# Turning the third weight of a feed-forward block in 32x32 blocks on VectorE instead of on TensorE

## The chip, the core and the metric

The kernel runs on one core of a Trainium2 chip. The core has five engines that run at the same time, each with its own list of instructions in a fixed order: TensorE (PE in the profile; its weight loads are PEld), VectorE (DVE), ScalarE (ACT), GpSimd (POOL) and SyncE (SP), which here only issues DMAs. They wait for each other through semaphores. The metric is the device time of one execution in microseconds.

## What is computed

A gated linear recurrence over 4 batches, 8 heads, 768 steps and head width 48, and then a feed-forward block on its output, x, of 3072 tokens by 384:

```python
for t in range(S):
    state = alpha[:, :, t, :, None] * state + np.einsum('bhd,bhe->bhde', k[:, :, t], v[:, :, t])
    y[:, :, t] = np.einsum('bhd,bhde->bhe', q[:, :, t], state)
...
a = x @ w1
b = x @ w2
h = a * b @ w3
return (h @ w_out).astype(np.float32)
```

w1 and w2 are 384 x 1024, w3 is 1024 x 1024, w_out is 1024 x 384. The four weights come to the kernel as 64-bit floats; everything else is 32-bit.

## The kernel before

**Stages.** The first part, until about 186 us, works the recurrence off in 24 chunks of 128 tokens (N) and stores x, transposed, to DRAM in eight groups of three chunks (`xd`). The second part, the gates, multiplies x by w1 and w2 for 8 groups of 384 tokens and 8 tiles of 128 of the 1024 columns, 64 gates in all, and stores each product ab to DRAM (`abd`). Twenty gates already run inside the first part (`early_gate`), the other 44 follow (`late_gate`). The third part (`project`, from about 370 us) loads ab again and multiplies it by one matrix of 1024 x 384. That matrix, `w3o`, is w3 times w_out: the kernel does not multiply ab by w3 and the result by w_out, it folds the two weights together first. The fold is done in eight steps of 128 rows of w3 (`fold(i)`), spread among the late gates.

**Products in three parts.** TensorE multiplies values cut to a short mantissa (FP32R), so each operand is split into parts h, l and m: h is the value rounded down by a ScalarE activation, l and m are what is left, made by two VectorE instructions. A product of K tiles takes 3 x K matmuls. `onto` does the first two parts into one PSUM bank, has ScalarE scale the bank in place (L535), and adds the third part later, when two more products have been begun (`pending`, `settle(keep)`). A late gate is two such products of nine matmuls each (KM = 3): the first is copied to a tile r by ScalarE (L567), and VectorE multiplies the second bank by r into ab (L571). r has two buffers, PSUM has eight banks.

**Weights.** `to_fp32` turns 64-bit floats into 32-bit ones by integer work. It loads a `raw` tile (four buffers) through SP's queue (L230), then ScalarE makes `rest` of the low words (L238) and `power` (L243), and VectorE does five instructions: two masks or shifts of the high words (L239, L242), two scalar_tensor_tensor (L245, L246) and a multiplication (L248). `load_out(j)` converts 128 rows of w_out and splits them into `wo` (L590 to L594), `load_w3(i, c0)` converts 128 rows by 512 columns of w3 into half of a tile `w3`, which has three buffers. These generators stand in a queue, `weights`; `fetch` starts the loads ahead and `convert` advances the conversions by a step or two at each gate. A DMA on a queue waits, before it is issued, until the eighth before it has landed, because eight semaphores go round.

**The fold.** A product with w3 contracts over w3's columns, while w3 lies with its rows on the partitions. So `fold(i)` first transposes 128 rows of w3: eight 128x128 transposes on TensorE into two PSUM banks (L612), from which ScalarE writes h (L614) and VectorE l and m (L615, L618) of `w3T`, a tile with a single buffer. Then `onto` multiplies w3T by wo: 16 matmuls for the first two parts, 8 for the third. `done` splits the result into w3o (L623 to L625).

**Order.** The Python loops give each engine's work, and a scheduler in the framework puts the instructions of every engine in a fixed order when the program is built. The main loop over `todo`, the list of gates, interleaves a gate, some steps of conversion and, once two loads of a fold's w3 are converted, that fold. Between the start of one fold's products and the next lie 54 matmuls of gates and 24 of the fold. Splits of x for the groups that come next (`split_x`, L502 to L504) stand in between, and the stores of ab and the loads of x go through GpSimd's queue in this part.

Of the kernel before, what the change touches and what calls it, by code (L numbers as in the profile page):

```python
# [10 lines left out]
FP32 = mybir.dt.float32  # L11
# [4 lines left out]
AF = mybir.ActivationFunctionType  # L16
ALU = mybir.AluOpType
# [3 lines left out]
P = 4096.0  # L21
# [27 lines left out]
def kernel(  # L49
# [12 lines left out]
    nc = tc.nc  # L62
    B, H, S, D = q.shape
    C = 128
    DM = H * D
    DF = moe_w1.shape[1]
    NCH = S // C
    N = B * NCH
    NP = H // 2
    DP = 64  # L70
    KM = DM // C
    KF = DF // C
    G = 3
# [2 lines left out]
    CW = 512  # L76
# [3 lines left out]
    TURNED = 8  # L80
    assert D <= DP and DM % C == 0 and DF % CW == 0 and S % C == 0 and N % G == 0
    assert DM <= 512 and TG <= 512

    def pool(name, bufs, stack=ctx, **kw):
        return stack.enter_context(tc.tile_pool(name=name, bufs=bufs, **kw))
# [19 lines left out]
    def bank():  # L105
        return ps.tile([C, 512], FP32, tag="bank", name="bank")

    st, mark = {}, {}
# [13 lines left out]

    vs = [p1.tile([C, H, DP], FP32, name=f"v{i}") for i in range(AHEAD + 1)]
    for x in vs:
        nc.gpsimd.memset(x[:, :, D:], 0.0)
    vts = [p1.tile([C, NP, DP], FP32, name=f"vt{i}") for i in range(2)]
    for x in vts:
# [35 lines left out]
    def turn_v(n):  # L163
        if turned(n):
            for half in range(2):
                nc.gpsimd.tensor_copy(out=vts[n % 2][ds(DP * half, DP), :, 0:D],  # L166
                                      in_=st["v", n][ds(DP * (1 - half), DP), 1::2, 0:D])

    spare = tr[0].tile([C, 3 * KM * TG], FP32R, tag="x3", name="x3")[:].bitcast(FP32)
    sums2 = spare[:, 0:4 * C].rearrange("p (e s t) -> p e s t", e=2, s=2)  # L170
# [11 lines left out]
    ident = const.tile([C, C], FP32, name="ident")  # L182
    rebias = const.tile([C, 1], FP32, name="rebias")

    w12 = [p.tile([C, 3, 2, KM, CW], FP32R, name=f"w12{i}") for i, p in enumerate((w12ap, const))]

# [5 lines left out]
    keep = p1.tile([C, C], I32, name="keep")  # L192
    keep_turned = p1.tile([C, 2, DP], I32, name="keep_turned")
    qks = [p1.tile([C, 2, H, DP], FP32, name=f"qk{i}") for i in range(3)]
# [27 lines left out]
    for x in Ts + decs:  # L222
        nc.gpsimd.memset(x, 0.0)

    def to_fp32(dst, *srcs):

        n, m = len(srcs) * srcs[0].shape[1], srcs[0].shape[1]
        raw = rawp.tile([C, n], I64, tag="raw", name="raw")
        for i, src in enumerate(srcs):
            nc.sync.dma_start(out=raw[:, ds(i * m, m)], in_=src)  # L230
        yield
        words = raw.bitcast(U32).rearrange("p (n w) -> p n w", w=2)
        low, high = words[:, :, 0], words[:, :, 1]

        mant = cvt.tile([C, n], FP32, tag="mant", name="mant")
        top = mant.bitcast(U32)
        rest = cvt.tile([C, n], FP32, tag="rest", name="rest", bufs=2)
        nc.scalar.activation(rest, low, AF.Copy, scale=2.0 ** -52)  # L238
        nc.vector.tensor_scalar(top, high, 0x000FFFFF, 0x00100000, op0=ALU.bitwise_and, op1=ALU.bitwise_or)  # L239

        power = cvt.tile([C, n], U32, tag="power", name="power", bufs=2)
        nc.vector.tensor_scalar(power, high, 20, 0x7FF, op0=ALU.logical_shift_right, op1=ALU.bitwise_and)  # L242
        nc.scalar.activation(power, power, AF.Relu, scale=2.0 ** 23, bias=rebias)  # L243
        yield
        nc.vector.scalar_tensor_tensor(mant, top, 2.0 ** -20, rest, op0=ALU.mult, op1=ALU.add)  # L245
        nc.vector.scalar_tensor_tensor(power, high, 0x80000000, power, op0=ALU.bitwise_and, op1=ALU.bitwise_or)  # L246
        to = mant if dst is None else dst()
        nc.vector.tensor_mul(to, mant, power.bitcast(FP32))  # L248
        yield
        return to  # L250

    def load_gates(i, kk, half):
        w = yield from to_fp32(None, (moe_w1, moe_w2)[i][ds(kk * C, C), ds(half * CW, CW)])
        h, l, m = (w12[half][:, x, i, kk, :] for x in range(3))
        nc.scalar.activation(h, w, AF.Copy, scale=(1.0 - 2.0 ** -13) / P)
        yield
        mark["l"] = nc.vector.scalar_tensor_tensor(l, h.bitcast(FP32), -P, w, op0=ALU.mult, op1=ALU.add).ins
        done.append((i, kk, half))
        if half:
            nc.vector.scalar_tensor_tensor(m, h.bitcast(FP32), P + 1.0, w, op0=ALU.mult, op1=ALU.subtract)  # L260
        else:
            thirds.append((m, h, l))

    weights, begun, thirds, done = deque(), deque(), deque(), []
# [229 lines left out]
    def load_x(g, queue=nc.sync):  # L494
        st["xT", g] = xp.tile([C, KM, TG], FP32, tag="xT", name="xT")
        queue.dma_start(out=st["xT", g], in_=xd[g].rearrange("(k p) t -> p k t", p=C))

    def split_x(g, i):
        x = st.pop(("xT", g))
        t = tr[i].tile([C, 3 * KM * TG], FP32R, tag="x3", name="x3").rearrange("p (s k t) -> p s k t", s=3, k=KM)  # L500
        st["x3", g] = t
# [29 lines left out]
    def onto(w, x, width, done, keep):  # L531

        p, n = bank()[:, 0:width], len(w[0])
        products(p, w, x, (0, 1), n, True, True)
        nc.scalar.activation(p, p, AF.Copy, scale=1.0 + 1.0 / P)  # L535

        def end():
            products(p, w, x, (2,), n, False, True)
            done(p)

        pending.append(end)
        settle(keep)

    def factors(g, f):
        x = [[st["x3", g][:, part, kk, :] for kk in range(KM)] for part in range(3)]
        half, at = divmod(f * C, CW)
        return [([[w12[half][:, part, i, kk, ds(at, C)] for kk in range(KM)] for part in range(3)], x)
                for i in range(2)]
# [36 lines left out]
            (nc.gpsimd if late else nc.sync).dma_start(out=abd[g][:, f, :], in_=ab)  # L585

    def load_out(j):
        w = yield from to_fp32(None, moe_w_out[ds(j * C, C), :])
        h, l, m = (wo[:, part, j, :] for part in range(3))
        nc.scalar.activation(h, w, AF.Copy, scale=1.0 - 2.0 ** -13)  # L590
        nc.vector.tensor_sub(w, w, h.bitcast(FP32))
        yield
        nc.scalar.activation(l, w, AF.Copy, scale=P)
        nc.vector.scalar_tensor_tensor(m, w, -P, h.bitcast(FP32), op0=ALU.mult, op1=ALU.add)  # L594

    def load_w3(i, c0):
        def to():
            if ("w3", i) not in st:
                st["w3", i] = foldp.tile([C, DF], FP32, tag="w3", name="w3", bufs=3)
            return st["w3", i][:, ds(c0, CW)]  # L600
        yield from to_fp32(to, moe_w3[ds(i * C, C), ds(c0, CW)])
        if c0 + CW == DF:
            folds.append(fold(i))

    def fold(i):
        w3 = st.pop(("w3", i))
        w3T = foldp.tile([C, 3, KF, C], FP32R, tag="w3T", name="w3T")
        rest = []
        for part in range(2):
            tp = bank().rearrange("p (j c) -> p j c", c=C)  # L610
            for j in range(KF // 2):
                nc.tensor.transpose(tp[:, j, :], w3[:, ds((part * KF // 2 + j) * C, C)], ident)  # L612
            h, l, m = (w3T[:, x, part * KF // 2:(part + 1) * KF // 2, :] for x in range(3))
            nc.scalar.activation(h, tp, AF.Copy, scale=1.0 - 2.0 ** -13)  # L614
            nc.vector.tensor_sub(l, tp, h.bitcast(FP32))  # L615
            rest.append((m, h, tp))
        for m, h, tp in rest:
            nc.vector.scalar_tensor_tensor(m, h.bitcast(FP32), -1.0 - 1.0 / P, tp, op0=ALU.mult, op1=ALU.add)  # L618
        yield True

        def done(po):
            h, l, m = (w3o[:, part, i, :] for part in range(3))
            nc.scalar.activation(h, po, AF.Copy, scale=(1.0 - 2.0 ** -13) / P)  # L623
            nc.vector.scalar_tensor_tensor(l, h.bitcast(FP32), -P, po, op0=ALU.mult, op1=ALU.add)
            nc.vector.scalar_tensor_tensor(m, h.bitcast(FP32), P + 1.0, po, op0=ALU.mult, op1=ALU.subtract)  # L625

        onto(*([[x[:, part, j, :] for j in range(KF)] for part in range(3)] for x in (w3T, wo)), DM, done, 2)
# [37 lines left out]
    for half in range(DF // CW):  # L665
        for kk in range(KM):
            weights.extend(load_gates(i, kk, half) for i in range(2))
# [21 lines left out]
    for n in range(N + 1):  # L689
# [89 lines left out]
        if n == N - 3:  # L779
            while begun:  # L780
                convert(1)
            weights.extend(load_out(j) for j in range(KF))
            fetch(4)
# [7 lines left out]
    foldp = pool("foldp", 1, stack=folding, reuse_waits="tile")  # L791
# [1 line left out]
    w3o = None  # L793
    folds, folded = deque(), 0
    for i in range(KF):
        for c0 in range(0, DF, CW):
            weights.append(load_w3(i, c0))

    todo, order = list(fill), []
    low, high = range(FH), range(FH, KF)  # L800
# [74 lines left out]
```

## Time and profile before

| what | value |
|---|---|
| device time, median of 3 runs | 474.79 us (471.58, 474.79, 475.42) |
| span of the profiled execution | 471.2 us |
| TensorE busy | 453.1 us (96%), 4360 matmuls |
| VectorE busy | 363.5 us (77%), 610 instructions |
| ScalarE busy | 278.9 us (59%), 552 instructions |
| mean granted TensorE clock | 0.996 |

The page divides the span into 40 slices of 11.8 us and gives each engine's busy share in tenths, the clock that TensorE was granted and the share of the 16 DMA engines that was in use:

```profile
PE   4996999999999999999999999999999999999996
...
DVE  2876997999979898999999968764542977766771
ACT  4864975767767554889787656554553633333330
...
PEclk9999999999999999999999999999999999999999
DMA  9999999999999953566685433212013886555511
```

Slice 17 begins at 188 us, where the late gates do; the eight folds lie in slices 22 to 30. TensorE is full from the second slice to the last but one, except for the fourth, VectorE all but full to slice 23, and the DMA engines only in the first 14.

The waits and the groups of the profile are read as follows. A group is a line of the kernel with an engine, an operation and shapes; its mean is the duration of one instruction, and on TensorE and VectorE the next one can begin before it has ended. The idle time of a group is what its engine stood still just before it, with what ended most of that time. The chain of waits goes back from the last instruction: to what released it, or else to the instruction before it on its engine.

### The profile page before, as it was taken

Reading aid. Unit: us, or ns where it says so; the run is one execution under the profiler, and the core shown is the slowest. Engines: PE = TensorE matmul, PEld = TensorE weight load, DVE = VectorE, ACT = ScalarE, POOL = GpSimd, SP = SyncE. Lnnn points to the kernel's source line nnn. Section 1 sums busy time; section 2 is a strip of 40 time slices with the busy share of each in tenths; the row PEclk is TensorE's granted clock in tenths of the full one; section 3 lists DMA queues with packets and bytes.
Section 4 is the critical chain, followed back from the end, with each engine's and each line's share of the span. In section 5 each row is a group of like instructions: output and inputs, shape, how many; then the busy total and the mean of one; then the engine's idle time right before and its main releaser. Section 6 shows DMA issues by size and latency. Waiting matters only on the chain.

```text
span 471.2 us, 11168 instructions
## 1 busy us (share of the span) xinstructions
PE 453.1 (96%) x4360; PEld 430.4 (91%) x4360; DVE 363.5 (77%) x610; ACT 278.9 (59%) x552; POOL 96.0 (20%) x186
## 2 busy tenths in 40 slices
PE   4996999999999999999999999999999999999996
PEld 2675889898999989999999999999999999999996
DVE  2876997999979898999999968764542977766771
ACT  4864975767767554889787656554553633333330
POOL 6332243234313550222221111111011000000000
PEclk9999999999999999999999999999999999999999
DMA  9999999999999953566685433212013886555511
GB/s 182 251 189 247 239 226 207 222 218 207 203 207 209 266 141 116 170 185 220 205 297 190 133 124 101 85 50 85 35 51 111 245 243 184 176 160 167 173 52 50
DMA packets 145668, 80.36 MB, mean 171 GB/s; under 512 B 96240, under 2 KB 137456, under 8 KB 145616
## 3 DMA queue, kind: packets, MB, share of 16 engines
q1 hardware_dynamic: 139840, 64.44, 55.2%
q0 software_dynamic: 5776, 15.22, 10.3%
q8 instruction: 34, 0.56, 0.5%
q14 instruction: 18, 0.15, 0.1%
HBM read 57.58 MB, written 22.06 MB: 169 GB/s over the span
## 4 chain that ended last, share of the span: by engine, by line
PE 86%; DMA 5%; DVE 4%; ACT 3%; issue 1%; SPq 0%; DVEq 0%; ACTq 0%
PE bank L510 70%; DMA kq<-in_q_dram 3%; PE bank L425 3%; PE bank L376 2%; PE bank L477 2%; PE bank L469 2%; PE bank L612 1%; PE bank L388 1%; PE bank L338 1%; PE bank L341 1%; DMA raw<-in_moe_w_dram 1%; PE bank L480 1%; DVE qk L354 1%; PE bank L414 1%; PE bank L449 1%
## 5 line engine op out<-in xcount | busy, mean ns | idle before, releaser
L510 PE MATMUL bank<-x,w 128*128 128x384 f32 x1152 | 212.4, 338 | 1.9 <-DVE ms L435 0.9
L510 PEld LDWEIGHTS bank<-x,w 128*128 128x128 f32 x1152 | 199.9, 188 | 4.4 <-DVE ms L435 1.0
L510 PE MATMUL bank<-w3o,ab 128*128 128x384 f32 x576 | 100.2, 336 | 0.0
L510 PEld LDWEIGHTS bank<-w3o,ab 128*128 128x128 f32 x576 | 99.8, 188 | 0.0
L535 ACT ACTIVATE bank<-bank 128x384 f32<-128x384 f32 x96 | 45.6, 476 | 43.0 <-PE bank L510 42.8
L519 ACT ACTIVATE t<-bank 128x384 f32<-128x384 f32 x64 | 31.6, 495 | 54.8 <-PE bank L510 54.6
L585 POOL DMA_DIRECT2D abd<-ab x45 | 25.7, 570 | 143.4 <-DVE ab L571 126.8
L571 DVE TENSOR_TENSOR ab<-bank,r 128x384 f32<-128x384 f32 x44 | 24.4, 555 | 25.6 <-ACT bank L535 16.4
L378 ACT COPY qkT<-bank 128x512 f32<-128x512 f32 x48 | 26.0, 591 | 24.2 <-PE bank L376 24.2
L641 DVE TENSOR_TENSOR ab<-abl,ab 128x1024 fp32r<-128x1024 f32 x24 | 29.4, 1224 | 13.0 <-ACT ab L640 13.0
L640 ACT ACTIVATE ab<-abl 128x1024 fp32r<-128x1024 f32 x24 | 25.5, 1061 | 20.2 <-PE bank L510 18.0
L510 PE MATMUL bank<-wo,w3T 128*128 128x384 f32 x192 | 35.9, 334 | 0.0
L354 DVE TENSOR_TENSOR qk<-kq,e 128x768 f32<-128x768 f32 x24 | 23.3, 971 | 15.0 <-ACT e L345 7.5
L510 PEld LDWEIGHTS bank<-wo,w3T 128*128 128x128 f32 x192 | 33.5, 188 | 0.0
L243 ACT ACTIVATE power<-power,rebias 128x512 uint32<-128x512 uint32 (+1 forms) x36 | 25.1, 700 | 12.2 <-DVE power L242 12.1
L521 DVE SCALAR_TENSOR_TENSOR o<-bank,t 128x384 f32<-128x384 f32 x24 | 13.4, 557 | 22.4 <-issue 13.7
L642 DVE SCALAR_TENSOR_TENSOR ab<-ab,abl 128x1024 fp32r<-128x1024 f32 x24 | 29.2, 1219 | 0.0
L521 DVE SCALAR_TENSOR_TENSOR r<-bank,t 128x384 f32<-128x384 f32 x40 | 22.1, 552 | 6.8 <-ACT t L519 4.1
L245 DVE SCALAR_TENSOR_TENSOR mant<-mant,rest 128x512 f32<-128x512 uint32 (+1 forms) x36 | 23.6, 655 | 2.0 <-ACT rest L238 1.9
L238 ACT ACTIVATE rest<-raw 128x512 f32<-128x512 uint32 (+1 forms) x36 | 23.4, 652 | 1.0 <-DMA raw<-in_moe_w_dram 1.0
L166 POOL COPY vt<-v 64x192 f32<-64x192 f32 x32 | 19.4, 606 | 22.0 <-DMA v<-in_v_dram 21.0
L246 DVE SCALAR_TENSOR_TENSOR power<-raw,power 128x512 uint32<-128x512 uint32 (+1 forms) x36 | 23.3, 655 | 0.3 <-ACT power L243 0.2
(104 smaller groups left out, 685.9 us busy)
## 6 DMA issues: line engine op xcount, KB each, us to landing
raw<-in_moe_w_dram SPq DMA_DIRECT2D x28, 512.0 KB, 5.3
abl<-abd SPq DMA_DIRECT2D x24, 512.0 KB, 4.3
abd<-ab POOLq DMA_DIRECT2D x45, 192.0 KB, 3.1
xT<-xd POOLq DMA_DIRECT2D x9, 576.0 KB, 4.4
kq<-in_k_dram SPq DMA_DIRECT2D x24, 192.0 KB, 5.0
kq<-in_q_dram SPq DMA_DIRECT2D x24, 192.0 KB, 5.8
xd<-x SPq DMA_DIRECT2D x48, 96.0 KB, 3.9
out_dram<-o SPq DMA_DIRECT2D x24, 192.0 KB, 3.4
```

The costliest lines, as they stand in the source:

```text
L243: nc.scalar.activation(power, power, AF.Relu, scale=2.0 ** 23, bias=rebias)
L354: mark["qk", n] = nc.vector.tensor_mul(qks[n % 3][:, :, :, 0:D], st.pop(("kq", n)), st.pop(("e", n)).rearrange("p i (h d) -> p i h d", h=H ...
L378: mark["qkT", n] = nc.scalar.copy(qkT[:, :, :, ds(DP * half, DP)], tp[half]).ins
L510: nc.tensor.matmul(p, w[part][i], x[part][i], start=start and part == parts[0] and i == 0, stop=stop and part == parts[-1] and i == n - 1, ...
L519: nc.scalar.activation(t, p1, AF.Copy, scale=(1.0 + 1.0 / P) * scale)
L521: nc.vector.scalar_tensor_tensor(to, p2, scale, t, op0=ALU.mult, op1=ALU.add)
L535: nc.scalar.activation(p, p, AF.Copy, scale=1.0 + 1.0 / P)
L571: nc.vector.tensor_mul(ab, p, r[0])
L585: (nc.gpsimd if late else nc.sync).dma_start(out=abd[g][:, f, :], in_=ab)
L640: nc.scalar.activation(t[:, 0], ab, AF.Copy, scale=1.0 - 2.0 ** -13)
L641: nc.vector.tensor_sub(t[:, 1], ab, t[:, 0].bitcast(FP32))
L642: nc.vector.scalar_tensor_tensor(t[:, 2], t[:, 0].bitcast(FP32), -1.0 - 1.0 / P, ab, op0=ALU.mult, op1=ALU.add)
```

## The change

w3 is no longer transposed on TensorE. VectorE can turn a tile in blocks: each block of 32 partitions by 32 columns is transposed for itself, and stays on its 32 partitions. To make whole rows and columns out of that, the load has to place the right columns on the right 32 partitions beforehand.

- `load_w3(i, u)` now loads 64 rows of w3 with all 1024 columns, instead of 128 rows with 512. The columns come in four quarters of 256; quarter r goes to the partitions 32 r to 32 r + 31, in a DMA of its own (32 partitions x 2 x 256 values of 64 bits, 128 KB). A raw tile of 128 x 512 thus takes four DMAs instead of one, 64 in all instead of 16.
- After the conversion, VectorE turns the tile of 128x512 in one instruction (16 in all) into half of a tile `w3` that already has w3's columns on the partitions: [128, 8, 128].
- In that tile, partition 32 r + p of tile j holds column 256 r + 32 j + p. So the rows of w_out have to come in the same order: `load_out(j)` loads its 128 rows as four pieces of 32 rows that are 256 rows apart, in four DMAs instead of one, 32 in all instead of 8. The product over w3's columns is the same sum in another order.
- `fold(i)` loses the 64 transposes and reads `w3` straight from SBUF: one ScalarE activation and two VectorE instructions of 128x1024, instead of two and four of 128x512 from PSUM.
- `to_fp32` loses the argument `dst`: it always returns the tile `mant`.

```diff
+    Q = 32
...
-    def to_fp32(dst, *srcs):
+    def to_fp32(*srcs, width=None):
 
-        n, m = len(srcs) * srcs[0].shape[1], srcs[0].shape[1]
+        n = width or sum(src.shape[1] for src in srcs)
         raw = rawp.tile([C, n], I64, tag="raw", name="raw")
         for i, src in enumerate(srcs):
-            nc.sync.dma_start(out=raw[:, ds(i * m, m)], in_=src)
+            if width:
+                rows = ds(i * src.shape[0], src.shape[0])
+                to = raw[rows] if len(src.shape) == 2 else raw[rows].rearrange("p (b c) -> p b c", b=src.shape[1])
+            else:
+                to = raw[:, ds(i * src.shape[1], src.shape[1])]
+            nc.sync.dma_start(out=to, in_=src)
...
-        to = mant if dst is None else dst()
-        nc.vector.tensor_mul(to, mant, power.bitcast(FP32))
+        nc.vector.tensor_mul(mant, mant, power.bitcast(FP32))
         yield
-        return to
+        return mant
...
     def load_out(j):
-        w = yield from to_fp32(None, moe_w_out[ds(j * C, C), :])
+        rows = moe_w_out.rearrange("(r j p) m -> j r p m", p=Q, j=KF)[j]
+        w = yield from to_fp32(*(rows[r] for r in range(C // Q)), width=DM)
...
-    def load_w3(i, c0):
-        def to():
-            if ("w3", i) not in st:
-                st["w3", i] = foldp.tile([C, DF], FP32, tag="w3", name="w3", bufs=3)
-            return st["w3", i][:, ds(c0, CW)]
-        yield from to_fp32(to, moe_w3[ds(i * C, C), ds(c0, CW)])
-        if c0 + CW == DF:
+    def load_w3(i, u):
+        rows = moe_w3[ds(i * C + u * DP, DP), :].rearrange("(b p) (r c) -> r p b c", p=Q, r=C // Q)
+        w = yield from to_fp32(*(rows[r] for r in range(C // Q)), width=CW)
+        if ("w3", i) not in st:
+            st["w3", i] = foldp.tile([C, KF, C], FP32, tag="w3", name="w3", bufs=3)
+        to = st["w3", i][:, :, ds(u * DP, DP)].rearrange("p j (b c) -> p b j c", c=Q)
+        nc.vector.transpose(to, w.rearrange("p (b j c) -> p b j c", b=DP // Q, c=Q))
+        if u:
             folds.append(fold(i))
 
     def fold(i):
         w3 = st.pop(("w3", i))
         w3T = foldp.tile([C, 3, KF, C], FP32R, tag="w3T", name="w3T")
-        rest = []
-        for part in range(2):
-            tp = bank().rearrange("p (j c) -> p j c", c=C)
-            for j in range(KF // 2):
-                nc.tensor.transpose(tp[:, j, :], w3[:, ds((part * KF // 2 + j) * C, C)], ident)
-            h, l, m = (w3T[:, x, part * KF // 2:(part + 1) * KF // 2, :] for x in range(3))
-            nc.scalar.activation(h, tp, AF.Copy, scale=1.0 - 2.0 ** -13)
-            nc.vector.tensor_sub(l, tp, h.bitcast(FP32))
-            rest.append((m, h, tp))
-        for m, h, tp in rest:
-            nc.vector.scalar_tensor_tensor(m, h.bitcast(FP32), -1.0 - 1.0 / P, tp, op0=ALU.mult, op1=ALU.add)
+        h, l, m = (w3T[:, x] for x in range(3))
+        nc.scalar.activation(h, w3, AF.Copy, scale=1.0 - 2.0 ** -13)
+        nc.vector.tensor_sub(l, w3, h.bitcast(FP32))
+        nc.vector.scalar_tensor_tensor(m, h.bitcast(FP32), -1.0 - 1.0 / P, w3, op0=ALU.mult, op1=ALU.add)
         yield True
...
     for i in range(KF):
-        for c0 in range(0, DF, CW):
-            weights.append(load_w3(i, c0))
+        weights.extend(load_w3(i, u) for u in range(2))
```

More of the change, by code (lines that the diff above doesn't have):

```diff
@@ L246, in to_fp32 @@
         nc.vector.scalar_tensor_tensor(power, high, 0x80000000, power, op0=ALU.bitwise_and, op1=ALU.bitwise_or)
-        to = mant if dst is None else dst()
-        nc.vector.tensor_mul(to, mant, power.bitcast(FP32))
+        nc.vector.tensor_mul(mant, mant, power.bitcast(FP32))
         yield
-        return to
+        return mant
     def load_gates(i, kk, half):
-        w = yield from to_fp32(None, (moe_w1, moe_w2)[i][ds(kk * C, C), ds(half * CW, CW)])
+        w = yield from to_fp32((moe_w1, moe_w2)[i][ds(kk * C, C), ds(half * CW, CW)])
         h, l, m = (w12[half][:, x, i, kk, :] for x in range(3))
```

## The prediction

> **What bounds the kernel now.** I read the chain of waits in order of time first, then busy time by stretch, then the groups by line and shape, then VectorE's timeline. The chain (start, length, what, count):
>
> ```profile
> 185.94 62.29 PE bank L510 x354
> 248.23 0.87 PE bank L612 x8
> 249.10 13.53 PE bank L510 x78
> 262.63 0.87 PE bank L612 x8
> ...
> 349.10 0.87 PE bank L612 x8
> 349.97 117.59 PE bank L510 x678
> 467.63 0.56 DVE o L521
> ```
>
> From 185.94 to 467.56 us the chain is TensorE alone, matmul on matmul. Asked for TensorE's waits from 186 to 467, the trace names none. Eight pieces are L612, the transposes of the third weight, one per fold, each 0.87 us. So what is taken off TensorE here shortens the run, as long as the engines that feed it keep up. The one near its limit shows in busy time by stretch (us from the start, length, then busy time and count of PE, PEld, DVE, ACT, POOL, and clock, DMA share, GB/s):
>
> ```profile
> 190.00:248.00 58.00, 58.00 (x332) 58.00 (x331) 57.65 (x111) 50.46 (x104) 13.89 (x22) 1.00 0.68 217
> 248.00:262.60 14.60, 14.60 (x90) 14.53 (x89) 13.84 (x24) 11.00 (x21) 2.55 (x4) 1.00 0.52 182
> 291.50:305.90 14.40, 14.40 (x88) 14.36 (x87) 11.71 (x19) 8.82 (x16) 2.39 (x4) 1.00 0.24 83
> 334.70:349.10 14.40, 14.40 (x88) 14.36 (x87) 7.62 (x11) 7.30 (x14) 1.62 (x3) 1.00 0.12 42
> ```
>
> VectorE is full until 248 and has room from then on, 2.7 us of 14.4 at 291.5 and 6.8 at 334.7. The change gives it sixteen more instructions. The rows that price it (line, engine, op, tiles, shapes, count, busy, mean ns, idle before):
>
> ```profile
> L612 PE MATMUL bank<-ident,w 128*128 128x128 f32 x64 | 8.3, 272 | 0.0
> L615 DVE TENSOR_TENSOR w3T<-bank,w3T 128x512 fp32r<-128x512 f32 x16 | 10.3, 683 | 0.9 <-ACT w3T L614 0.9
> L641 DVE TENSOR_TENSOR ab<-abl,ab 128x1024 fp32r<-128x1024 f32 x24 | 29.4, 1224 | 13.0 <-ACT ab L640 13.0
> L248 DVE TENSOR_TENSOR w<-mant,power 128x512 f32<-128x512 f32 x16 | 11.0, 686 | 1.0 <-PE bank L612 1.0
> ```
>
> **Taken off TensorE.** 64 transposes in eight groups, 8 x 0.87 = 7.0 us (109 ns each, their spacing on the chain; the 272 ns of the row is a duration that overlaps the next). The built program of the changed kernel has 64 fewer instructions on TensorE, and what is left stands in the same order, so nothing replaces them. Worth -7.0 us.
>
> The Trainium skill, in "VectorE: DVE Perf Modes", section "Rules for kernel authors", speaks against the change: a 128x128 transpose belongs on TensorE where PSUM will do. Its section on the three transpose paths has 390 ns on TensorE and 311 ns on VectorE for 128 columns of bf16; that would make an estimated 25 us saved and 4 x 311 ns = 1.24 us per new instruction, where this trace spaces TensorE's at 109 ns.
>
> **The transposes on VectorE.** Sixteen of 128x512 f32, SBUF to SBUF. No row shows one. From below: L239, one input of 128x512, 443 ns. From above: four times L248, 2.74 us, if the rearranging takes several passes. I take L248's 0.69 us, one pass of the same shape and type through SBUF. What counts on a full engine is the spacing, which the timeline gives:
>
> ```profile
> 188.44 0.55 DVE L248 TENSOR_TENSOR mant<-mant,power 128x384 f32<-128x384 f32 x1
> 188.91 0.55 DVE L245 SCALAR_TENSOR_TENSOR mant<-mant,rest 128x384 f32<-128x384 uint32 x1
> 189.38 0.56 DVE L521 SCALAR_TENSOR_TENSOR r<-bank,t 128x384 f32<-128x384 f32 x1
> ```
>
> Rows of 0.55 us stand 0.47 apart, so 0.08 of each overlaps: 0.60 for 128x512, 1.14 for 128x1024, 1.27 for L503 and L504, 0.34 for L239 and L242. The transposes add 16 x 0.60 = 9.6 us.
>
> **Does VectorE keep up?** Per fold TensorE will need 78 x 0.1735 = 13.53 us. VectorE's work per fold: two loads of w3, each 2 x 0.34 + 4 x 0.60 = 3.08 with the transpose, so 6.16; split of w3T, now two of 128x1024, 2.28 (before, four of 0.60); two of w3o at 0.47, 0.94; three products ab at 0.47, 1.41; five splits of x in six folds, 5/6 x 2.54 = 2.1. Sum 12.9 of 13.53. It fits by 0.6 us. Order matters too, so I added up the changed kernel's own VectorE list from the product at 190.31 on. The same sum over the kernel before puts the tenth product after it at 31.95 us and the trace at 32.67 (222.98 + 0.47 - 190.78), so it is good to 3%. In the changed kernel the sum reaches product 10 at 32.1, hence no later, and product 20 at 61.6 against 65.3: the first fold's split now stands some 13 us ahead of its use. From product 10 to 34 there are 89.5 us of work, fifteen transposes among it. TensorE reaches product 34 at 319.2 (started at 324.38 before, less six groups of 0.87), so it gives 96.0 us for it from 223.2. Spare: 6.5 us, so a transpose may be spaced 0.60 + 6.5/15 = 1.03 us without VectorE falling behind. With 0.60 no product lags TensorE by over 0.9 us; before, product 25 started at 283.50, 2.5 after TensorE had it ready by the count of matmuls, and cost nothing. What is queued behind a late VectorE is ab: ab frees r, which has two buffers, so ScalarE can wait two gates of 3.1 us less the 1.6 from r to ab, 4.6 us, before TensorE lacks a scaled bank. I take 0.
>
> **The split of w3T.** One tile w3T: ScalarE may write fold k+1 only after the third part of fold k (eight matmuls) is through. Then come 36 gate matmuls, 6.2 us, and eight more (1.4) before the second part is read. Needed: w3o's 0.49 on ScalarE, h at 1.06 (L640's shape), sub at 1.22: 2.8 us. 4.8 us are left; before, the sub ended at 251.03 and its part was read from 252.06 + 8 x 0.1735 = 253.45, 2.4 us later. ScalarE's h now waits for the second transpose instead of for TensorE, and behind h on ScalarE are the bank scalings that TensorE's third parts wait for; but in VectorE's list the second transpose stands at least 9 us of work ahead of the split. Cost 0. Also gone is L248's wait for TensorE, 1.0 us, now inside the sum.
>
> **The loads.** 24 loads of 128 partitions become 96 of 32, issued by SP. A DMA issue of L230 takes 0.33 us, so a full tile goes out about 1.0 to 1.3 us later, after which it lands in 2.9 to 6.6 us (5.1 in the median). Worst 0.1 + 1.3 + 6.6 = 8 us. By the sums above a freed raw buffer is needed again 11.6 us later at the soonest; so at least 3.6 us cover it, and if that cover went, the delay would fall on VectorE's list with its 4.6 us. The queue also waits, before each issue, for the eighth DMA before it to land: two tiles per landing of about 5 us, one in 2.5, while one is wanted per 6.8 us from 252 on. Moved past: around 159 to 176 us SP's stores of xd and ab and one load of v stand behind up to nine more issues. The load of v was issued at 161.75 and slips about 0.8 us, one store of ab goes from 164.95 to some 170. That v is wanted two steps later, and its buffer of ab three gates later, at 183. Bounds for all loads: -1 us (an ab store less in the way of a load) to +4 us (the largest part of 1.3 us showing at the three places where L238 waited for raw); I take 0: the last transfer in the chain of waits is a load of raw that ends at 91.3 us. GpSimd's list does not change.
>
> The Trainium skill, "SBUF — State Buffer", section "Can I just issue two DMAs to hit both halves?", speaks against it too: only one transfer over 128 partitions reaches all 16 ports. With that page's 2 us plus bytes over 218 GB/s for 32 partitions I estimate four quarters at 4.4 us against 3.2 for one; no row here shows a quarter.
>
> **Sum.** 471.2 - 7.0 = 464.2 us of span. The timed runs have a median of 474.79 (471.58 to 475.42), 3.6 above that span, so I take the step off the median: 467.8 us.
>
> **Rivals.**
> (a) VectorE cannot turn a block in one pass: slower. Place: products 10 to 34, 223 to 319 us. Fifteen transposes spaced p make it 15 x (p - 1.03) late, of which 4.6 is hidden; the gain is gone at 7.0 + 4.6 = 11.6 late, p = 1.80 us. With four passes, p = 2.40, it is 20.6 late, 16 on the path: 467.8 + 16 = 484 us. For it: no row shows the instruction, and VectorE was full up to 248. Against: one 32-bit input, and every one-pass row of this size costs 0.44 to 0.73. With two passes, 1.20, 2.6 us late, all hidden.
> (b) The quarters come late: no change. If a landing took 16 us, SP's eight in flight would bring a tile in 8, and wanted is one in 6.8; over the twelve w3 tiles left after the first four that is 12 x 1.2 = 14.4 us, less the 3.6 and 4.6 that cover it: 6.2 lost, 474.0 us. For it: raw was used within 5 us of its issue around 240. Against: the DMA share is 0.68 and falls to 0.24, and the changed list asks for raw later.
> (c) The change does not do what it says (transposes stay on TensorE): 474.8; the built program has none left, so I give it no chance of its own.
>
> **How the numbers follow.** Forecast 0.72; (a), with the weaker cases that leave some gain, 0.15, of which 0.10 ends slower; (b) and small losses around the handover at 160 to 186, 0.13. One per cent is about 4.75 us, what a measurement here can tell from no change: under 470.0 is faster. The forecast's own range is 463.8 to 469.5: the lowest run less 7.0 is 464.6, less 0.8 of the loads' 1 us; the highest is 468.4, plus 1.1 us of lag. Upwards I add 3.5 for half of (b) and for the part of (a) that leaves some gain: 473.0. Faster 0.72, within 1% 0.17, slower 0.11.
>
> **What the next profile would show.** Right: no L612-like row; the chain one run of L510 from about 186 to about 460; the new VectorE row 0.6 to 0.8 us x16; ab starting within 1 us of TensorE; TensorE without waits from 186 on. Wrong: a VectorE transpose row over 1.1 us with ScalarE's or TensorE's waits on ab or r between 223 and 320; or L238 and L239 idle on raw with SP's landings over 10 us.

## The result and the profile after

| | before | changed |
|---|---|---|
| device time, median of 4 runs each | 473.8 us (471.58 to 475.42) | 465.51 us (464.52 to 468.57) |
| ratio | | 0.9854, 95% interval 0.9822 to 0.9887 |
| span of the profiled execution | 471.2 us | 464.1 us |
| timed again later | 471.99 us | 463.80 us, ratio 0.9826 (0.9800 to 0.9852) |

The change is faster by 1.5%, and the span of the profiled execution is 0.1 us from the sum of the prediction, 464.2. That it is so near is partly luck: the changed kernel profiled once more had a span of 462.3 us. The chain of waits of the changed kernel from 186 us on, in order of time:

```profile
185.94 274.48 PE bank L515 x1578
460.41 0.04 DVEq L526
460.45 0.04 issue
460.49 0.56 DVE o L526
```

L515 is the matmul line that was L510. What were seventeen pieces, matmuls broken by eight groups of transposes, is now one piece, and in these two profiled runs it begins at the same 185.94 us. From there to the last matmul it took 467.56 - 185.94 = 281.6 us before and takes 274.5 now, 7.1 less. The trace names no wait of TensorE between 186 and 467.

The groups that answer to the ones which priced the change (line, engine, op, tiles, shapes, count, busy, mean ns, idle before):

```profile
L608 DVE STREAM_TRANSPOSE w<-mant 128x512 f32<-128x512 f32 x16 | 11.3, 706 | 0.1
L617 DVE TENSOR_TENSOR w3T<-w,w3T 128x1024 fp32r<-128x1024 f32 x8 | 9.8, 1220 | 0.0
L253 DVE TENSOR_TENSOR mant<-mant,power 128x512 f32<-128x512 f32 x28 | 19.2, 687 | 0.5
```

The new instruction takes 706 ns, as good as one pass of a two-input instruction of that shape, L253's 687. Its spacing shows in VectorE's timeline around the third fold:

```profile
283.81 0.70 DVE L608 STREAM_TRANSPOSE w<-mant 128x512 f32<-128x512 f32 x1
284.43 0.65 DVE L252 SCALAR_TENSOR_TENSOR power<-raw,power 128x512 uint32<-128x512 uint32 x1
...
289.65 0.55 DVE L576 TENSOR_TENSOR ab<-bank,r 128x384 f32<-128x384 f32 x1
```

It is 0.62 us, where the sum had 0.60. The last line is product 27 (the products ab of the late gates, counted as in the prediction), the one latest against TensorE in the stretch of the folds by the count of matmuls: TensorE had it ready at 288.82, 0.83 us earlier. How full VectorE is, by stretches of one fold (columns as in the prediction):

```profile
190.00:248.00 58.00, 58.00 (x332) 58.00 (x331) 56.90 (x105) 47.38 (x98) 13.41 (x22) 1.00 0.66 200
248.00:261.50 13.50, 13.50 (x80) 13.50 (x79) 11.06 (x20) 9.46 (x19) 2.26 (x4) 1.00 0.53 167
261.50:275.00 13.50, 13.50 (x80) 13.50 (x79) 12.97 (x22) 8.38 (x17) 1.96 (x4) 1.00 0.53 165
275.00:288.50 13.50, 13.50 (x80) 13.50 (x79) 13.41 (x21) 9.38 (x18) 2.72 (x4) 1.00 0.58 161
288.50:302.00 13.50, 13.50 (x80) 13.50 (x79) 12.69 (x22) 9.52 (x19) 2.39 (x4) 1.00 0.42 134
302.00:315.50 13.50, 13.50 (x80) 13.50 (x79) 13.43 (x22) 9.42 (x18) 2.40 (x4) 1.00 0.12 44
315.50:329.00 13.50, 13.50 (x79) 13.50 (x79) 9.06 (x15) 6.68 (x14) 1.84 (x4) 1.00 0.26 89
329.00:342.50 13.50, 13.50 (x80) 13.50 (x79) 7.41 (x10) 7.12 (x14) 1.62 (x3) 1.00 0.12 44
```

VectorE is now close to full until 315, not 248, but for the stretch from 248.0 to 261.5: most of the room that the kernel before had there is used up. TensorE is busy throughout all the same. A row at 99% looks like the bound of the kernel, and is not: as TensorE has no wait, what VectorE does there is done before TensorE wants it.

### The profile page after: what moved, and what is told of

The parts are those of the page before. It is cut to its first block, busy times and chain, and to the rows that moved or that the text cites. A ratio compares the mean times of both kernels' runs of the same rounds, so it can differ in the third digit from the quotient of the medians.

```text
span 464.1 us, 11153 instructions
## 1 busy us (share of the span) xinstructions
PE 446.0 (96%) x4296; PEld 424.3 (91%) x4296; DVE 371.1 (80%) x610; ACT 276.3 (60%) x544; POOL 94.3 (20%) x186
## 4 chain that ended last, share of the span: by engine, by line
PE 87%; DVE 5%; DMA 4%; issue 2%; ACT 1%; SPq 0%; DVEq 0%
PE bank L515 71%; DMA kq<-in_q_dram 4%; PE bank L381 3%; PE bank L430 2%; PE bank L474 2%; PE bank L482 2%; PE bank L454 1%; PE bank L393 1%; PE bank L343 1%; PE bank L346 1%; PE bank L485 1%; PE bank L419 1%; DVE ms L457 1%; DMA ac<-in_alpha_dram 1%; DVE x L509 1%
## 5 line engine op out<-in xcount | busy, mean ns | idle before, releaser
L515 PE MATMUL bank<-x,w 128*128 128x384 f32 x1152 | 209.5, 337 | 1.0 <-DVE ms L440 0.9
L515 PEld LDWEIGHTS bank<-x,w 128*128 128x128 f32 x1152 | 200.2, 188 | 2.8 <-DVE ms L440 1.2
L515 PE MATMUL bank<-w3o,ab 128*128 128x384 f32 x576 | 100.2, 336 | 0.0
L515 PEld LDWEIGHTS bank<-w3o,ab 128*128 128x128 f32 x576 | 99.9, 188 | 0.0
L515 PE MATMUL bank<-wo,w3T 128*128 128x384 f32 x192 | 35.9, 334 | 0.0
L515 PEld LDWEIGHTS bank<-wo,w3T 128*128 128x128 f32 x192 | 33.5, 188 | 0.0
L526 DVE SCALAR_TENSOR_TENSOR o<-bank,t 128x384 f32<-128x384 f32 x24 | 13.4, 557 | 22.7 <-issue 13.7
L253 DVE TENSOR_TENSOR mant<-mant,power 128x512 f32<-128x512 f32 (+1 forms) x36 | 23.6, 656 | 0.5
```

Source lines behind the costliest of these rows:

```text
L515: nc.tensor.matmul(p, w[part][i], x[part][i], start=start and part == parts[0] and i == 0, stop=stop and part == parts[-1] and i == n - 1, ...
L526: nc.vector.scalar_tensor_tensor(to, p2, scale, t, op0=ALU.mult, op1=ALU.add)
```

## The experiments

The theory: the gain is the 64 instructions that TensorE no longer has, and what was added to VectorE and to SP's queue lies wholly beside TensorE's work. Against it stood that the gain comes from the new path of the fold, that VectorE or the quarter loads cost something, and that VectorE is at its edge. Each timed kernel is compared with the kernel before on its own chip. The stretch from the start of TensorE's unbroken work to its last matmul, read from the chain of waits, tells them apart best:

| kernel | stretch, us | starts at | time, us | ratio to before (95%) |
|---|---|---|---|---|
| before | 281.6 | 185.94 | 473.8 | |
| changed | 274.5 | 185.94 | 465.51 | 0.9854 (0.9822 to 0.9887) |
| transposes back on TensorE | 281.9 | 186.20 | 473.09 | 1.0007 (0.9985 to 1.0029) |
| quarter loads alone | 281.6 | 184.75 | 472.74 | 1.0023 (0.9997 to 1.0049) |
| no turning on VectorE | 274.5 | 184.94 | 464.79 | 0.9858 (0.9822 to 0.9894) |
| turning done twice | 274.5 | 185.74 | 465.34 | 0.9859 (0.9829 to 0.9888) |
| turning done three times | 275.4 | 187.81 | 465.82 | 0.9880 (0.9840 to 0.9920) |
| turning done four times | 288.2 | 187.43 | 480.75 | 1.0204 (1.0144 to 1.0263) |
| whole loads | 274.5 | 185.16 | 464.51 | 0.9845 (0.9819 to 0.9871) |
| changed, again | 274.5 | 184.10 | 463.80 | 0.9826 (0.9800 to 0.9852) |

**The transposes back on TensorE.**

```diff
         w3T = foldp.tile([C, 3, KF, C], FP32R, tag="w3T", name="w3T")
+        for part in range(2):
+            tp = bank().rearrange("p (j c) -> p j c", c=C)
+            for j in range(KF // 2):
+                nc.tensor.transpose(tp[:, j, :], w3[:, part * KF // 2 + j, :], ident)
```

> The changed kernel with the 64 transposes put back on TensorE at their old places in its order, into PSUM banks that nobody reads; VectorE's transposes and the quarter loads stay. Theory (the gain is TensorE's 64 instructions, 109 ns each, and nothing else): eight pieces of 0.87 us come back into the chain, the span is 464.1 + 7.0 = 471.1 us, and the time is that of the kernel before within 0.5%. Rival (the gain, or part of it, comes from the new path: no PSUM banks for the fold, no wait of ScalarE for the transposes, another order on VectorE): the time stays near the changed kernel, span 464 to 467.

Measured: ratio 1.0007, and the whole gain is gone. The chain of waits of this kernel has the eight pieces again:

```profile
248.49 0.87 PE bank L618 x8
249.36 13.53 PE bank L515 x78
262.89 0.87 PE bank L618 x8
```

Nothing reads these transposes, and VectorE's path, the SBUF source of the fold and the quarter loads are those of the changed kernel. So the 64 instructions account for all of the gain, and the new path of the fold for none that can be measured.

**The quarter loads alone**, in the kernel before.

```diff
+        step = C // 4 if split else C
         for i, src in enumerate(srcs):
-            nc.sync.dma_start(out=raw[:, ds(i * m, m)], in_=src)
+            for p0 in range(0, C, step):
+                nc.sync.dma_start(out=raw[ds(p0, step), ds(i * m, m)], in_=src[ds(p0, step)])
```

> The kernel before with one part of the change alone: every load of w3 and of w_out in four DMAs of 32 partitions (the same data to the same places, transposes on TensorE). Theory (the quarters are covered by the raw buffers): TensorE stays without waits from 186 us on, span 471 within 1 us, time within 0.3% of the kernel before. Rival (quarters land late or hold SP's queue): VectorE and ScalarE idle on raw, above all around 234 to 249 us, where a tile was used within 5 us of its issue; 1 to 4 us slower.

Measured: ratio 1.0023, with 1 just inside the interval; the stretch is 281.6 as before, without a wait of TensorE. The interval leaves up to 2.3 us open, and a partition's 512 values come in one piece here, in two of 256 in the change; the next to last experiment takes up both. Landing, by the trace's list of issues (line and tiles, queue, count, KB each, median us to landing), before and here:

```profile
raw<-in_moe_w_dram SPq DMA_DIRECT2D x16, 512.0 KB, 4.5
```

```profile
raw<-in_moe_w_dram SPq DMA_DIRECT2D x64, 128.0 KB, 3.2
```

A quarter lands in 3.2 us, and SP issues the four of a tile some 0.46 us apart. Taken tile by tile, the last quarter is there 5.0 us after the first was issued (the median of the 16 tiles from 186 to 300 us), half a microsecond later than a whole load. Nothing shows that this is felt: ScalarE waited for raw for 1.0 us after 186 us in the kernel before, and does not at all here.

**No turning on VectorE.** The final multiplication writes the tile `w3` itself; w3 is folded unturned.

```diff
-            nc.vector.tensor_mul(mant, mant, power.bitcast(FP32))
+            nc.vector.tensor_mul(dst(), *(x.rearrange("p (b j c) -> p b j c", b=DP // Q, c=Q) for x in (mant, power.bitcast(FP32))))
...
-        nc.vector.transpose(to, w.rearrange("p (b j c) -> p b j c", b=DP // Q, c=Q))
```

> The changed kernel without the sixteen transposes on VectorE: the last multiplication of the conversion writes w3's tile directly, so w3 is folded without being turned (that part of the computation is left out). VectorE does 16 x 0.60 = 9.6 us less. Theory (VectorE's added work is hidden wholly): the same time as the changed kernel within 0.3%, span 464.1 within 0.7, VectorE's busy time 11 us lower. Rival (VectorE lagged a little and cost something): 1 to 3 us faster than the changed kernel.

Measured: the stretch is the same to 0.01 us, 274.48; the ratio is 0.9858, against 0.9854 for the changed kernel, and the span's 1.0 us lies before the stretch, at its start (184.94 against 185.94). VectorE's busy time fell from 371.1 to 362.4 us, by 8.7 where 11 were forecast. The sixteen instructions, which last 11.3 us added up, cost nothing on the path.

**The turning done two, three and four times.** The same edit with 2, 3 and 4:

```diff
-        nc.vector.transpose(to, w.rearrange("p (b j c) -> p b j c", b=DP // Q, c=Q))
+        for _ in range(2):
+            nc.vector.transpose(to, w.rearrange("p (b j c) -> p b j c", b=DP // Q, c=Q))
```

> The changed kernel with each of VectorE's sixteen transposes done twice in a row (same source, same place), as if one took 1.2 us. By the sums of the prediction VectorE then falls 15 x (1.20 - 1.03) = 2.6 us behind, all of it hidden by r's two buffers (4.6 us). Theory: the same time as the changed kernel, span 464 to 465, products ab starting up to 3 us after TensorE has them ready. Rival (VectorE is at its edge, and the tie of VectorE and TensorE is tighter than r's two buffers say): TensorE waits for r, ab or w3T between 223 and 320 us, 3 to 9 us slower than the changed kernel.

Measured: the stretch is 274.47. Twice is free, as expected, but not for the reason given. VectorE was not 2.6 us behind: from product 10 to product 42 no product starts more than 0.9 us after TensorE has it ready, no later than in the changed kernel, so r's two buffers had nothing to hide.

> The changed kernel with each of VectorE's sixteen transposes done three times in a row, as if one were spaced 1.80 us. The prediction put the point at which the whole gain is gone here: 15 x (1.80 - 1.03) = 11.6 us late, 4.6 hidden, 7.0 on the path. Theory: span 464.1 + 7.0 = 471 us, the time of the kernel before; TensorE waits between 250 and 320 us. Rival (more is hidden than r's two buffers give: VectorE's later room and the scheduler's other order take it up): under 468. Rival the other way (late folds hold TensorE in order): over 474.

Measured: ratio 0.9880, the stretch 0.9 us longer, where 7 were forecast: a miss. The first rival, that VectorE's later room and the scheduler's other order take it up, is what came; its span, 466.9, is under the rival's 468. Of TensorE's lists only the weight loads name a wait in the stretch (engine, line, what it waited for, us in total, times, longest):

```profile
PEld bank L515 <- ACT w3T L617: 1.0, 3, 0.3
```

> The changed kernel with each of VectorE's sixteen transposes done four times in a row, as if one were spaced 2.40 us. By the prediction's sum 15 x (2.40 - 1.03) = 20.6 us late, 16 on the path: span 480 us, 1.4% slower than the kernel before. Rival (more is hidden): under 474. The step from three to four, 15 x 0.60 = 9 us, should show in full on the path, since by then VectorE sets the pace.

Measured: ratio 1.0204, the stretch 13.7 us longer than the changed kernel's, for 16 forecast; the span is 479.3 for 480. But the step from three to four is 12.8 us, not 9, and the wait is another than the one named. In the waits of TensorE and of ScalarE from 186 us on (the same columns):

```profile
PE bank L515 <- ACT w3T L617: 8.9, 3, 4.2
```

```profile
ACT w3T L617 <- DVE w L609: 2.0, 2, 1.2
```

TensorE does not run out of banks or r because ab is late. It stands before the fold's first matmul, for h of w3T (L617), and h in turn, at two folds, for the second turned half (L609, the transposes). The chain of this kernel shows the alternation directly, from VectorE's transposes to ScalarE's h to TensorE:

```profile
311.05 12.77 PE bank L515 x72
...
326.07 0.62 DVE w L609
326.69 0.57 DVE power L252
327.26 0.63 DVE w L609
327.92 1.07 ACT w3T L617
329.03 14.36 PE bank L515 x72
...
346.42 12.28 PE bank L515 x60
```

The lines of matmuls show a second cost. TensorE stood three times for h; the 72 matmuls after the first time took 12.77 us, the 72 after the second 14.36, and the 60 after the third 12.28, where the first pace gives 10.64. The clock that TensorE was granted was lower in those last two (stretches of this kernel, columns as in the table of VectorE's stretches above, the clock third from the end):

```profile
302.00:329.00 27.00, 20.09 (x115) 19.45 (x113) 26.62 (x46) 15.35 (x28) 3.69 (x6) 1.00 0.43 143
329.00:356.00 27.00, 24.99 (x124) 24.50 (x125) 25.18 (x40) 12.11 (x22) 2.15 (x4) 0.87 0.08 30
```

So of the 13.7 us some 3.2 are a slower TensorE and not a wait. In the traces with one, two and three transposes the clock from 190 us to 350 us is 1.00. Why it was lower after two of the three times is not shown.

Why three fit: the prediction's sum took the changed kernel's list and made its transposes longer. The built program of a kernel with more transposes has another list. With the same spacings (0.62 a transpose), I counted in the four lists (the traces hold the same instructions) how much VectorE work lies between product 10 and product 34, for which TensorE gives 96.0 us: 89.8 with one transpose, 94.2 with two, 96.9 with three, 98.1 with four. With three, 36 of the 48 transposes lie ahead of product 34, with one 15 of 16: the last folds' turning has been moved behind, where VectorE was busy 7.4 of 13.5 us in the changed kernel. By the three-fold list's sum product 34 is 2.0 us late and product 37 is 3.0; the trace has them 2.0 and 2.6 later than in the changed kernel, after the starts of the stretches are taken off. With four, product 37 is due after 118.8 us of work in 109.3 of TensorE, 9.5 late: 20.7 us of work now stand between 34 and 37, for 13.3 of TensorE. Those 9.5 and the 3.2 of the slower clock make 12.7 of the 13.7 us measured. So the sum was right as a method, and wrong in holding the list fixed. How a slower instruction in the changed kernel's own list would do could not be tried this way, since each added instruction changes the list.

**Whole loads**, in the changed kernel.

```diff
-        w = yield from to_fp32(*(rows[r] for r in range(C // Q)), width=CW)
+        w = yield from to_fp32(moe_w3[ds(i * C, C), ds(u * CW, CW)])
```

(and the same for w_out.)

> The changed kernel with whole loads: one DMA of 128 partitions for each tile of w3 (128 rows by 512 columns) and of w_out, in the old order of rows and columns, so that the folded weight is not the one asked for (the placing of the quarters is left out); conversions, VectorE's transposes and folds as in the changed kernel. Theory (the quarters cost nothing): the same time as the changed kernel within 0.3%. Rival (the quarters cost the 0.2% that the quarters alone hinted at, 1.0023 with an interval that just holds 1): 1 to 2 us faster than the changed kernel, most of it before TensorE's unbroken stretch begins, at about 186 us.

Measured: 464.51 us, against 463.80 for the changed kernel timed with it, and the stretch is 274.5. A whole load lands in 3.8 us here, while the last quarter of a tile lands 4.9 us after the first was issued in the changed kernel (medians from 186 to 300 us). The quarters cost nothing that shows in the time; the hint of the second experiment was not confirmed.

> The changed kernel itself, timed again beside the whole loads on the same chip. Its span should be 1.7 us below its time, as in its first runs; the step against the kernel before should be 7.0 us, a ratio of 0.985. If the true step is larger (the first runs gave 8.3 by medians), something besides the 64 transposes was taken off.

Measured: ratio 0.9826, a step of 8.2 us by the medians; 0.985 is just inside the interval. Its span, 462.3, is 1.7 below its time (463.96 us for the profiled run). The stretch is again 274.5. So 7.1 us of the step are placed. Whether the last microsecond is real stays open: if it is, it lies ahead of the stretch. The start of the stretch differs by more than that between profiled executions: it is 184.75 to 186.20 in kernels with the transposes on TensorE, and 184.10 to 185.94 in those without them and with at most two passes on VectorE. With three and four passes it is 187.81 and 187.43; whether those passes delay it is not shown.

## Why the prediction was right

- **What comes off TensorE**: 7.0 us forecast, 7.1 in the stretch. The spacing on the chain (0.87 us for eight) was the right price. The row's mean of 272 ns would have given 17.4.
- **VectorE's price**: 0.60 taken, 0.62 found. The bounds reached to 2.74, and the choice of the nearest one-pass row was right.
- **VectorE keeps up**: 12.9 of 13.53 us per fold forecast; the trace has 12.69 to 13.43 busy of 13.5 in the four stretches from 261.5 to 315.5. "No product lags TensorE by over 0.9 us" held with 0.83 in the folds; before them product 13 lags by 1.0, and it does so without the turning too (the last two products, 43 and 44, start 1.7 and 1.9 after, behind splits of ab for the third part, as in the kernel before, where product 43 had 2.0).
- **The split of w3T and the loads**: no cost, shown by the whole loads, the quarters alone and the unbroken stretch. The store of ab that was forecast to slip from 164.95 to some 170 went out at 171.1; the load of v, forecast to slip by 0.8 from 161.75, went out at 164.20, 2.45 later, of which 1.1 us were there before the quarters' issues.
- **The sum**: the span 464.2 was right to 0.1, partly by luck: what was forecast is the step, and the stretch happened to begin at 185.94 in both profiled runs, while it began anywhere from 184.10 to 186.20 in the others with at most two passes. The predicted median, 467.8, was 2.3 above the measured one, and this is the term that was mis-sized: "3.6 above that span" took the distance between three runs' median and one run's span for something that lies around the span. The profiled runs show what does: 465.8 - 464.1 = 1.7 us. With it the sum was 464.2 + 1.7 = 465.9.
- **Rival (a)** named the right engine and the right stretch, and its end was near (480.75 us for 484), but by another mechanism: the cover is first the room in the list behind product 34, and r's two buffers only after it (with three passes product 37 starts 2.6 us later than in the changed kernel, and TensorE does not wait for r), and what is late in the end is the fold's h, not ab. That the end was near is partly luck, since TensorE's waits are 8.9 us and some 3.2 more come from the lower clock, which was no part of the sum. The point at which the gain is gone lies between three and four passes, not at three.

## What to carry to other kernels

When one engine's chain has no gaps, price an instruction that leaves it by its spacing on the chain, not by its duration, and price the one that takes its place by the room on its new engine until its result is wanted. A busy share near 100% on the helper does not say that it is late: compare the times at which its results are ready and wanted. And where a scheduler builds the lists, "how much longer could this instruction be" is answered from the list that it would build, since it moves work into any room that is left.

## What the runs showed of the hardware that was not expected

- VectorE transposes 128x512 f32 in 32x32 blocks in 706 ns, within 3% of a multiplication of that shape (687), though it writes its blocks 512 bytes apart; four times in a row it is still 701 ns each.
- Four loads of 32 partitions are all there 4.9 to 5.0 us after the first was issued (changed kernel, quarters alone), one of 128 in 3.8 to 4.5 us (whole loads, kernel before): 0.4 to 1.2 us between them. The estimate from the Trainium skill's page "SBUF — State Buffer" that stood in the prediction, 4.4 us for four against 3.2 for one, has both 0.5 to 1.3 us too short, and a difference, 1.2 us, at the upper end of that.
- With four passes TensorE stood for 8.9 us, and in the stretch from 329 to 356 us, after the second and third time, its granted clock was 0.87, against 1.00 in the stretch before.
